# An FFT filter and an MLP on one core: where the forward second stage keeps its sums, and what its four filter products read

## The chip, the cores and the metric

The kernel runs on one core of a Trainium2 chip. The metric is the time of one execution in device microseconds (us), taken as the median of several runs. The time before is 2332.32 us, the median of 3 runs (2330.84 to 2332.87).

## The reference

Two things are computed one after the other. The first is a filter in the frequency domain along the sequence, for 8 batches of 3008 positions and 256 columns. The second is an MLP with 2048 hidden units on the resulting 24064 rows:

```python
def _attn_ref(x, filt_r, filt_i):
    X = np.fft.rfft(x, axis=1)
    F = (filt_r + 1j * filt_i)[None, :, :]
    y = np.fft.irfft(X * F, n=x.shape[1], axis=1)
    return y.astype(np.float32)

def _moe_ref(x, w_in, w_out):
    h = x @ w_in
    g = h * (1.0 / (1.0 + np.exp(-1.702 * h)))
    return (g @ w_out).astype(np.float32)
```

All arrays are float32. The weights of the MLP come as float64 and are converted on the chip.

## The kernel before

**Split numbers.** TensorE multiplies in float32r. To keep the precision, a value is split in a high half (ScalarE's copy rounded to float32r) and a low half (value less high half), and a product is made of the three products high x high, high x low, low x high.

**The transform.** 3008 = 64 x 47, so that the Fourier transform of one batch is done in two stages and the way back in two more. Stage 1 of batch b (`fft(b)`, lines 519 to 555) takes the input in 6 slices and writes `a_d` in DRAM. The second stage, `forward(i)` and `backward(i)` for i from 0 to 15 (lines 602 to 639), takes slice i of `a_d` (tile `zy`, high halves on 48 of 64 partitions in one half of the tile, low halves in the other), transforms it, multiplies it with the filter and transforms it back. The last stage belongs to the tiles of the MLP (below).

`forward(i)` works on two halves k = 0, 1 (real and imaginary part; `sides(k)` gives the 48 partitions h of the half, 0 to 47 or 64 to 111, and the 48 partitions o of the other half). `second(i, ..., k)` is one matmul that leaves two parts of the sum on the partitions h and o of one PSUM tile of 128x512. `merge` brings them together: ScalarE copies the part on o into the SBUF tile `c_buf` on h (L599), and VectorE adds the part on h, from PSUM, into `c_buf` (L600). Then four products with the filter `f_buf` are made: k = 0 times the imaginary part into `u_buf` (L608), k = 1 times the negative imaginary part into `u_buf` (L613), and both halves times the real part in one operation on 112 partitions (L614). GpSimd adds the two (L615), VectorE and GpSimd split the result in high and low half in `zy` (L619, L620). `backward(i)` does the same matmuls and merges with the inverse table, into the SBUF tile `b`, and every second one sends `b` to DRAM (`b_d`, L636) on ScalarE's queue.

**The MLP.** There are 48 tiles (b, t), six of each batch, of 512 columns (t = 5 of an even batch: 384), and each runs 16 chunks fc of 128 hidden units. A chunk has 6 matmuls into `h` (`first`, L844), two gelus of ScalarE, the first into `gh` in SBUF (L848), the second in place in PSUM (L849), VectorE's difference `gl` (L850), and 6 matmuls into `o` (`second` of `mlp`, L869). The 6 matmuls into `h` read the tile's `y` in high half (4 of them) and low half (2).

**Where a tile comes from.** `y` of tile (b, t) is made by `turned_signal`: load `br` from `b_d` (SyncE's queue), ScalarE's high halves `bh` and GpSimd's low halves `bl` (L785, L786), 6 matmuls, a transposition by VectorE, a trip through DRAM (`z_d`), and again high and low halves (L726, L727). That is so for t > 0 from batch 1 on and for t = 0 from batch 3 on; the other tiles go a shorter way (`signal`), and the tiles of batch 7 with t > 0 a packed one. Batch 0 has a transform of its own (`first_fft`), whose filter products (`product`, L457, L458) read a PSUM tile and the filter in SBUF. The load of `br` needs all 16 slices of the second stage of the batch, up to its last matmul, which the program names i2_b_15_1 (i2: way back, batch b, i = 15, k = 1). Names with s2 are the forward matmuls, s1 those of stage 1.

**PSUM.** Eight banks are shared by tags. `ring("f")` has three banks in turn for everything of the transforms, `ring("h")` two for `h`, `ps_o` has two for `o`, and `ps_x` is one that goes to "f" between chunks 32 and 95 of the whole program and to "h" after that.

**What sets the order.** The main loop runs over the chunks. Between chunks it advances the generators: `fft` of the next batch by a list of costs (`COSTS`, spread evenly over the chunks of one batch), and the generators of the next tiles by a table of due times. A scheduler that simulates a timeline then lays out each engine's instructions in one fixed order; matmuls given to `keep_in_program_order` (here those of the transforms) keep their order among themselves, others may move past them. On the chip each engine runs its list in that order and waits where an operand isn't there.

Of the kernel before, what the change touches and what calls it, by code (L numbers as in the profile page):

```python
# [14 lines left out]
ALU = mybir.AluOpType  # L15
# [6 lines left out]
Q = 112  # L22
# [147 lines left out]
def tile_kernel(  # L170
# [9 lines left out]
    nc = tc.nc  # L180
# [17 lines left out]
    def ring(kind, shape, name):  # L198

        own = {"f": (ps_f, 3), "h": (ps_h, 2)}[kind]  # L200
        turn_of[kind] += 1
        if shared[0] == kind and turn_of[kind] % (own[1] + 1) == 0:
            return ps_x.tile(shape, F32, tag="x", name=name)
        return own[0].tile(shape, F32, tag=kind, name=name)
# [99 lines left out]
    zy = []  # L304
# [157 lines left out]
    def fft(b):  # L462
# [111 lines left out]
        def load(i):  # L574
            for k in range(2):
                src = a_d[k, 4 * i : 4 * i + 4].rearrange("q n d -> n q d")
                nc.gpsimd.dma_start(zy[0][64 * k : 64 * k + 48, i % 2].rearrange("p k s d -> p (k s) d"), src)  # L577

        def load_f(i):
            for k in range(2):  # L580
                load_in(f_buf[64 * k : 64 * k + 48, 2 * (i % 2) : 2 * (i % 2) + 2], fs[i])

        def second(i, m, src, name, k):

            pin = tc.keep_in_program_order
            ps = ring("f", [P, 2, D], f"{name}_{b}_{i}_{k}")
            if i == 0:
                pin(nc.tensor.matmul(ps[:, 0], de_sb[:, k, m + 1], src[:, k, 0], start=True, stop=True))
                nc.tensor.matmul(ps[:, 1], de_sb[:, k, m], src[:, k, 1], start=True, stop=True)
            else:  # L590
                pin(nc.tensor.matmul(ps, de_sb[:, k, m], src[:, k], start=True, stop=True))  # L591
            return ps

        def sides(k):
            return slice(64 * k, 64 * k + 48), slice(64 - 64 * k, 112 - 64 * k)

        def merge(k, ps, dst):
            h, o = sides(k)
            nc.scalar.copy(dst[h], ps[o])  # L599
            nc.vector.tensor_tensor(dst[h], ps[h], dst[h], ALU.add)  # L600

        def forward(i):

            u1, u2 = c_buf[i % 3], u_buf[i % 2]
            fr = f_buf[:Q, 2 * (i % 2) : 2 * (i % 2) + 2]
            f_r, f_i = fr[:, :, 0, :], fr[:, :, 1, :]
            merge(0, second(i, 0, zy[0][:, i % 2], "s2", 0), u1)
            nc.vector.tensor_tensor(u2[64:Q], u1[0:48], f_i[0:48], ALU.mult)  # L608
            yield
            merge(1, second(i, 0, zy[0][:, i % 2], "s2", 1), u1)  # L610
            if i + 2 < 16:
                load(i + 2)
            nc.vector.scalar_tensor_tensor(u2[0:48], u1[64:Q], -1.0, f_i[64:Q], ALU.mult, ALU.mult)  # L613
            nc.vector.tensor_tensor(u1, u1[:Q], f_r, ALU.mult)  # L614
            nc.gpsimd.tensor_tensor(u1, u1, u2, ALU.add)  # L615
            y = zy[0][:, 2 + i % 2]
            for k in range(2):
                h, o = sides(k)
                nc.vector.tensor_copy(y[h, k], u1[h])  # L619
                nc.gpsimd.tensor_tensor(y[o, k], u1[h], y[h, k].bitcast(F32), ALU.subtract)  # L620
            if i + 2 < 16:
                load_f(i + 2)
            yield
# [24 lines left out]
        for i in range(17):  # L648
            if i < 16:
                yield from forward(i)  # L650
            if i:
                yield from backward(i - 1)
# [367 lines left out]
```

## Time and profile before

| | before |
|---|---|
| time, median of 3 runs | 2332.32 us (2330.84 to 2332.87) |
| the profiled execution | 2332.26 us, of which the span on the core 2330.2 us |
| granted clock of TensorE, mean | 1.00 |
| busy: TensorE | 2321.9 us, 100% |
| busy: VectorE | 1622.9 us, 70% |
| busy: ScalarE | 1458.4 us, 63% |
| busy: GpSimd | 1155.2 us, 50% |
| DMA | 293.44 MB, mean 126 GB/s |

PE is TensorE's matmuls, PEld its weight loads (which lie beside matmuls), DVE is VectorE, ACT ScalarE, POOL GpSimd, SP SyncE; ACTq and SPq are the queues on which these engines issue DMAs. A busy time is the sum of an engine's instructions over the span of 2330.2 us. L613 is line 613 of the kernel. "1155.2 x1019" is 1155.2 us in 1019 instructions. The profiled execution is one run of its own and stands 0.06 us from the median.

### The profile page before, as it was taken

What the parts mean: (1) busy time and instruction counts of PE and PEld (TensorE: products, weight loads), DVE (VectorE), ACT (ScalarE), POOL (GpSimd) and SP (SyncE); (2) the same over time, 40 slices, a digit from 0 to 9 for tenths busy, and PEclk for the clock granted to TensorE, in tenths of its full rate; (3) what the DMA queues carried; (4) which work ended last, traced back from release to release, by engine and by line L of the source; (5) the groups of instructions that cost most, each with busy time, mean ns of one, the idle gap of its engine ahead of it and who ended that gap; (6) DMA issues with size and microseconds to landing.
All of it is one profiled execution on the core that took longest, in us unless ns stands there. A gap on an engine that the chain in (4) does not pass through costs nothing.

```text
span 2330.2 us, 32285 instructions
## 1 busy us (share of the span) xinstructions
PE 2321.9 (100%) x10620; PEld 1942.6 (83%) x10620; DVE 1622.9 (70%) x2426; ACT 1458.4 (63%) x2686; POOL 1155.2 (50%) x1019
## 2 busy tenths in 40 slices
PE   9999999999999999999999999999999999999999
PEld 7888898888888889888888888988888888888887
DVE  7978876688666885678856887568876688633332
ACT  6666667666675666756676666766657566555553
POOL 3035546466564665556654555636647365422220
PEclk9999999999999999999999999999999999999999
DMA  9265545556455654555545554555655465421200
GB/s 340 82 193 110 111 107 143 133 136 134 108 148 128 144 136 131 152 121 138 133 133 141 130 128 121 148 136 128 138 133 143 115 141 121 111 62 55 82 28 19
DMA packets 191958, 293.44 MB, mean 126 GB/s; under 512 B 18736, under 2 KB 127920, under 8 KB 191792
## 3 DMA queue, kind: packets, MB, share of 16 engines
q1 hardware_dynamic: 115088, 180.89, 27.1%
q0 software_dynamic: 46592, 44.05, 11.6%
q10 hardware_dynamic: 30112, 66.44, 11.1%
q8 instruction: 85, 1.39, 0.3%
q14 instruction: 81, 0.66, 0.1%
HBM read 176.49 MB, written 114.82 MB: 125 GB/s over the span
## 4 chain that ended last, share of the span: by engine, by line
PE 95%; DVE 2%; DMA 2%; ACT 1%; issue 1%; ACTq 0%; POOL 0%; SPq 0%; DVEq 0%; POOLq 0%
PE h L844 43%; PE o L869 43%; PE i L591 2%; PE s L591 2%; PE s L540 1%; PE i L309 1%; PE i L307 1%; PE i L308 1%; PE i L709 1%; DMA x<-in_x_dram 0%; DVE gl L850 0%; PE s L388 0%; DVE w_tu L277 0%; DMA fs<-f_y 0%; DMA w<-in_w_out_dram 0%
## 5 line engine op out<-in xcount | busy, mean ns | idle before, releaser
L844 PE MATMUL h<-y,wi 128*128 128x512 f32 (+1 forms) x4608 | 1178.2, 385 | 0.6 <-DVE gl L850 0.5
L844 PEld LDWEIGHTS h<-y,wi 128*128 128x128 f32 x4608 | 858.9, 188 | 166.0 <-DVE gl L850 1.9
L850 DVE TENSOR_TENSOR gl<-h,gh 128x512 fp32r<-128x512 f32 (+1 forms) x768 | 521.3, 679 | 487.4 <-ACT h L849 452.9
L869 PE MATMUL o<-gh,wo 128*128 128x512 f32 (+1 forms) x3072 | 838.7, 385 | 0.8 <-ACT gh L848 0.8
L848 ACT ACTIVATE gh<-h 128x512 fp32r<-128x512 f32 (+1 forms) x768 | 452.7, 589 | 583.7 <-PE h L844 448.5
L869 PEld LDWEIGHTS o<-gh,wo 128*128 128x128 f32 x3072 | 573.4, 188 | 111.2 <-ACT gh L848 1.5
L869 PE MATMUL o<-gl,wo 128*128 128x512 f32 (+1 forms) x1536 | 481.7, 385 | 0.5 <-DVE gl L850 0.5
L849 ACT ACTIVATE h<-h 128x512 f32<-128x512 f32 (+1 forms) x768 | 448.4, 584 | 0.0
L620 POOL TENSOR_TENSOR zy<-c_buf,zy 48x512 fp32r<-48x512 f32 x224 | 316.3, 1412 | 75.0 <-DVE zy L619 62.7
L869 PEld LDWEIGHTS o<-gl,wo 128*128 128x128 f32 x1536 | 287.5, 188 | 56.4 <-DVE gl L850 1.2
L615 POOL TENSOR_TENSOR c_buf<-c_buf,u_buf 112x512 f32<-112x512 f32 x112 | 144.8, 1293 | 229.8 <-DVE c_buf L614 229.8
L577 POOL DMA_DIRECT2D zy<-a_d x224 | 130.7, 588 | 232.0 <-PE s L591 92.5
L786 POOL TENSOR_TENSOR bl<-br,bh 128x512 fp32r<-128x512 f32 x70 | 94.5, 1363 | 201.5 <-ACT bh L785 168.5
L600 DVE TENSOR_TENSOR c_buf<-s,c_buf 48x512 f32<-48x512 f32 x224 | 154.1, 688 | 34.0 <-ACT c_buf L599 29.4
L599 ACT COPY c_buf<-s 48x512 f32<-48x512 f32 x224 | 130.4, 582 | 70.8 <-PE s L591 57.6
L599 ACT COPY b<-i 48x512 f32<-48x512 f32 x224 | 130.4, 582 | 58.2 <-PE i L591 46.4
L600 DVE TENSOR_TENSOR b<-i,b 48x512 f32<-48x512 f32 x224 | 153.8, 687 | 15.1 <-ACT b L599 10.2
L543 DVE TENSOR_TENSOR a<-s,a 64x512 f32<-64x512 f32 x144 | 99.0, 688 | 61.9 <-ACT a L542 58.7
L619 DVE CAST zy<-c_buf 48x512 fp32r<-48x512 f32 x224 | 109.7, 490 | 39.1 <-POOL c_buf L615 34.1
L727 POOL TENSOR_TENSOR y<-y 128x512 fp32r<-128x512 f32 (+1 forms) x76 | 92.6, 1225 | 59.5 <-ACT y L726 48.1
L608 DVE TENSOR_TENSOR u_buf<-c_buf,f_buf 48x512 f32<-48x512 f32 x112 | 109.2, 975 | 3.8
L542 ACT CAST a<-s 64x512 fp32r<-64x512 f32 x144 | 83.8, 582 | 40.7 <-PE s L540 28.6
(138 smaller groups left out, 1867.4 us busy)
## 6 DMA issues: line engine op xcount, KB each, us to landing
f_buf<-fs SPq DMA_DIRECT2D x224, 192.0 KB, 3.5
zy<-a_d POOLq DMA_DIRECT2D x224, 192.0 KB, 3.7
a_d<-a ACTq DMA_DIRECT2D x144, 256.0 KB, 3.0
x<-in_x_dram SPq DMA_DIRECT2D x47, 512.0 KB, 5.5
br<-b_d SPq DMA_DIRECT2D x94, 256.0 KB, 4.5
out_dram<-out SPq DMA_DIRECT2D x43, 512.0 KB, 3.5
b_d<-b ACTq DMA_DIRECT2D x112, 192.0 KB, 2.8
z_d<-zt SPq DMA_DIRECT2D x40, 512.0 KB, 2.7
```

Of the source, the lines that this page charges most:

```text
L577: nc.gpsimd.dma_start(zy[0][64 * k : 64 * k + 48, i % 2].rearrange("p k s d -> p (k s) d"), src)
L599: nc.scalar.copy(dst[h], ps[o])
L600: nc.vector.tensor_tensor(dst[h], ps[h], dst[h], ALU.add)
L608: nc.vector.tensor_tensor(u2[64:Q], u1[0:48], f_i[0:48], ALU.mult)
L615: nc.gpsimd.tensor_tensor(u1, u1, u2, ALU.add)
L619: nc.vector.tensor_copy(y[h, k], u1[h])
L620: nc.gpsimd.tensor_tensor(y[o, k], u1[h], y[h, k].bitcast(F32), ALU.subtract)
L844: ins = nc.tensor.matmul(ps[:, :w], wi_sb[half][:, wk, kc, c], y[:, yk, kc, :w], start=n == 0, stop=n == 5)
L848: nc.scalar.activation(gh[:, :w], ps[:, :w], AF.Gelu_apprx_sigmoid)
L849: gelu.append(nc.scalar.activation(ps[:, :w], ps[:, :w], AF.Gelu_apprx_sigmoid).ins)
L850: nc.vector.tensor_tensor(gl[:, :w], ps[:, :w], gh[:, :w].bitcast(F32), ALU.subtract)
L869: ins = nc.tensor.matmul(pos[m][:, :w], wb[:, P * m : P * m + P], g[:, :w], start=first_one, stop=last_one)
```

## The change

`forward(i)` no longer calls `merge`. For each half, ScalarE copies the part on the other partitions into `c_buf` as before, but VectorE's sum now goes to the PSUM tile itself, over the part that it reads (L611 after). The four products are now four instructions of 48 partitions, two right behind each sum, and read the sum in PSUM and the filter in SBUF: times the imaginary part (L613 for k = 1, L615 for k = 0) and times the real part (L616), which replaces the one product on 112 partitions. The rest of the step (`load`, GpSimd's sum, the split, `backward`) is unchanged, though the load of the slice i + 2 is now asked for behind the products. Lines from 621 on of the kernel after are those of before plus 6.

```diff
--- before.py
+++ after.py
@@ -604,14 +604,20 @@
             u1, u2 = c_buf[i % 3], u_buf[i % 2]
             fr = f_buf[:Q, 2 * (i % 2) : 2 * (i % 2) + 2]
             f_r, f_i = fr[:, :, 0, :], fr[:, :, 1, :]
-            merge(0, second(i, 0, zy[0][:, i % 2], "s2", 0), u1)
-            nc.vector.tensor_tensor(u2[64:Q], u1[0:48], f_i[0:48], ALU.mult)
-            yield
-            merge(1, second(i, 0, zy[0][:, i % 2], "s2", 1), u1)
+            for k in range(2):
+                h, o = sides(k)
+                ps = second(i, 0, zy[0][:, i % 2], "s2", k)
+                nc.scalar.copy(u1[h], ps[o])
+                nc.vector.tensor_tensor(ps[h], ps[h], u1[h], ALU.add)
+                if k:
+                    nc.vector.scalar_tensor_tensor(u2[o], ps[h], -1.0, f_i[h], ALU.mult, ALU.mult)
+                else:
+                    nc.vector.tensor_tensor(u2[o], ps[h], f_i[h], ALU.mult)
+                nc.vector.tensor_tensor(u1[h], ps[h], f_r[h], ALU.mult)
+                if k == 0:
+                    yield
             if i + 2 < 16:
                 load(i + 2)
-            nc.vector.scalar_tensor_tensor(u2[0:48], u1[64:Q], -1.0, f_i[64:Q], ALU.mult, ALU.mult)
-            nc.vector.tensor_tensor(u1, u1[:Q], f_r, ALU.mult)
             nc.gpsimd.tensor_tensor(u1, u1, u2, ALU.add)
             y = zy[0][:, 2 + i % 2]
             for k in range(2):
```

In the lists of instructions, the rows below show operation, outputs <- inputs and shape. In them a name has the batch, the slice or chunk, and the half in it: s2_3_10_0 is the PSUM tile of batch 3, slice 10, half 0; h_2_5_7 is chunk 7 of tile (2, 5). The last number is a running one. "x4" is four alike in a row.

VectorE, forward step i = 10 of batch 3, before:

```order
L600 TENSOR_TENSOR c_buf1_83<-s2_3_10_0_7825,c_buf1_83 48x512
L608 TENSOR_TENSOR u_buf0_85<-c_buf1_83,f_buf_81 48x512
L850 TENSOR_TENSOR gl_2_3_12_7873<-h_2_3_12_7865,gh_2_3_12_7872 128x512
L600 TENSOR_TENSOR c_buf1_83<-s2_3_10_1_7848,c_buf1_83 48x512
L613 SCALAR_TENSOR_TENSOR u_buf0_85<-c_buf1_83,f_buf_81 48x512
L850 TENSOR_TENSOR gl_2_3_13_7901<-h_2_3_13_7893,gh_2_3_13_7900 128x512
L614 TENSOR_TENSOR c_buf1_83<-c_buf1_83,f_buf_81 112x512
```

The same step after:

```order
L611 TENSOR_TENSOR s2_3_10_0_7867<-s2_3_10_0_7867,c_buf1_83 48x512
L611 TENSOR_TENSOR s2_3_10_1_7891<-s2_3_10_1_7891,c_buf1_83 48x512
L615 TENSOR_TENSOR u_buf0_85<-s2_3_10_0_7867,f_buf_81 48x512
L616 TENSOR_TENSOR c_buf1_83<-s2_3_10_0_7867,f_buf_81 48x512
L613 SCALAR_TENSOR_TENSOR u_buf0_85<-s2_3_10_1_7891,f_buf_81 48x512
L616 TENSOR_TENSOR c_buf1_83<-s2_3_10_1_7891,f_buf_81 48x512
L856 TENSOR_TENSOR gl_2_3_15_8007<-h_2_3_15_7999,gh_2_3_15_8006 128x512
```

The products now hold the PSUM tile, here both sums stand ahead of them, and the step stands beside a later chunk of tile (2, 3).

TensorE, around the last matmul of the second stage of batch 3 (i2_3_15_1), before:

```order
L844 MATMUL h_2_5_1_8451<-y_2_5_7889,wi_0_583 128x384 x4
L869 MATMUL o_2_4_0_8069<-gl_2_4_14_8395,wo_1_984 128x512
L869 MATMUL o_2_4_0_8069<-gh_2_4_15_8422,wo_1_984 128x512
L591 MATMUL i2_3_15_1_8409<-zy_1451,de_sb_79 128x512
L869 MATMUL o_2_4_0_8069<-gh_2_4_15_8422,wo_1_984 128x512
```

The same matmul after:

```order
L875 MATMUL o_2_5_0_8543<-gh_2_5_4_8575,wo_0_584 128x384
L875 MATMUL o_2_5_1_8544<-gh_2_5_4_8575,wo_0_584 128x384
L850 MATMUL h_2_5_7_8644<-y_2_5_7932,wi_0_583 128x384 x4
L591 MATMUL i2_3_15_1_8457<-zy_1451,de_sb_79 128x512
L850 MATMUL h_2_5_7_8644<-y_2_5_7932,wi_0_583 128x384 x2
```

It stood among the matmuls of chunk 1 of tile (2, 5) and of the end of tile (2, 4); it stands within chunk 7 of tile (2, 5).

TensorE, where the first chunk of tile (3, 0) begins (h_3_0_0; its first 4 matmuls read the high half of y, the other 2 the low half), before:

```order
L540 MATMUL s1_4_2_1_8829<-e1_4_2_8752,t1_two_3258 128x512
L844 MATMUL h_3_0_0_8842<-y_3_0_8479,wi_0_583 128x512
L869 MATMUL o_2_5_0_8495<-gl_2_5_13_8769,wo_1_984 128x384
L869 MATMUL o_2_5_1_8496<-gl_2_5_13_8769,wo_1_984 128x384
L869 MATMUL o_2_5_0_8495<-gh_2_5_14_8788,wo_1_984 128x384
L869 MATMUL o_2_5_1_8496<-gh_2_5_14_8788,wo_1_984 128x384
L869 MATMUL o_2_5_0_8495<-gh_2_5_14_8788,wo_1_984 128x384
L869 MATMUL o_2_5_1_8496<-gh_2_5_14_8788,wo_1_984 128x384
L844 MATMUL h_3_0_0_8842<-y_3_0_8479,wi_0_583 128x512 x3
L844 MATMUL h_3_0_1_8868<-y_3_0_8479,wi_0_583 128x512 x4
```

After:

```order
L875 MATMUL o_2_5_0_8543<-gl_2_5_15_8867,wo_1_984 128x384
L875 MATMUL o_2_5_1_8544<-gl_2_5_15_8867,wo_1_984 128x384
L540 MATMUL s1_4_2_0_8848<-e0_4_2_8773,t1_two_3274 128x512
L540 MATMUL s1_4_2_1_8877<-e1_4_2_8800,t1_two_3274 128x512
L850 MATMUL h_3_0_0_8890<-y_3_0_8527,wi_0_583 128x512
L850 MATMUL h_3_0_1_8916<-y_3_0_8527,wi_0_583 128x512
L850 MATMUL h_3_0_2_8955<-y_3_0_8527,wi_0_583 128x512
L540 MATMUL s1_4_3_0_8940<-e0_4_3_8853,t1_two_3274 128x512
L850 MATMUL h_3_0_0_8890<-y_3_0_8527,wi_0_583 128x512 x3
L850 MATMUL h_3_0_1_8916<-y_3_0_8527,wi_0_583 128x512 x3
L850 MATMUL h_3_0_2_8955<-y_3_0_8527,wi_0_583 128x512 x3
L850 MATMUL h_3_0_0_8890<-y_3_0_8527,wi_0_583 128x512 x2
```

Before, the last two chunks of tile (2, 5) still stood around the first matmuls of tile (3, 0); after, tile (2, 5) is through, and three chunks of tile (3, 0) are begun with their high halves ahead of the first matmul on the low half. From i2_3_15_1 to that matmul there are, before, 20 matmuls of 512 columns and 172 of 384, and after, 17 and 118. On GpSimd, 16 operations stand before from the first bl of tile (3, 0) to its first L727 (L733 after), and 15 after; to the second one it is 17 in both.

The number of matmuls, of operations of ScalarE and GpSimd and of DMAs is unchanged; VectorE has 112 operations more.

## Rows read from the trace of the kernel before

**Rows 1.** Page, busy us (share of the span) and instructions, by engine.

```profile
PE 2321.9 (100%) x10620; PEld 1942.6 (83%) x10620; DVE 1622.9 (70%) x2426; ACT 1458.4 (63%) x2686; POOL 1155.2 (50%) x1019
```

**Rows 2.** TensorE's waits, first and last of 7: us, times, longest.

```profile
PE idle L328 <- DVE zero L375: 1.1, 1, 1.1
...
PE s L588 <- DMA zy<-a_d: 0.2, 1, 0.2
```

**Rows 3.** Window of the second stage: busy (instructions) by engine, PEclk, DMA share, GB/s.

```profile
1000.00:1145.00 145.00, 145.00 (x645) 120.16 (x644) 125.17 (x181) 91.99 (x166) 88.47 (x81) 1.00 0.59 133
```

**Rows 4.** VectorE by line and form: out<-in, count | busy us, mean ns | idle before.

```profile
L600 DVE TENSOR_TENSOR c_buf<-s,c_buf 48x512 f32<-48x512 f32 x224 | 154.1, 688 | 34.0 <-ACT c_buf L599 29.4
...
L608 DVE TENSOR_TENSOR u_buf<-c_buf,f_buf 48x512 f32<-48x512 f32 x112 | 109.2, 975 | 3.8
...
L613 DVE SCALAR_TENSOR_TENSOR u_buf<-c_buf,f_buf 48x512 f32<-48x512 f32 x112 | 88.8, 793 | 3.4
...
L614 DVE TENSOR_TENSOR c_buf<-c_buf,f_buf 112x512 f32<-112x512 f32 x112 | 85.2, 760 | 1.9
...
L457 DVE SCALAR_TENSOR_TENSOR u_buf<-s,f_y 48x512 f32<-48x512 f32 x8 | 5.5, 693 | 0.2
...
L458 DVE TENSOR_TENSOR u_buf<-s,f_y 48x512 f32<-48x512 f32 x8 | 5.5, 684 | 0.2
```

**Rows 5.** Page, costliest groups: ScalarE's gelu in place in PSUM.

```profile
L849 ACT ACTIVATE h<-h 128x512 f32<-128x512 f32 (+1 forms) x768 | 448.4, 584 | 0.0
```

**Rows 6.** TensorE's timeline at the start of batch 3: start, us, operation, count.

```profile
889.53 3.31 PE L844 MATMUL h<-y,wi 128*128 128x384 f32 x18
892.67 0.51 PE L869 MATMUL o<-gh,wo 128*128 128x384 f32 x2
...
922.49 1.78 PE L844 MATMUL h<-y,wi 128*128 128x512 f32 x7
924.10 0.51 PE L869 MATMUL o<-gl,wo 128*128 128x384 f32 x2
924.45 1.08 PE L844 MATMUL h<-y,wi 128*128 128x512 f32 x4
```

**Rows 7.** Timeline of all engines there; in brackets idle time before and its releaser.

```profile
887.91 0.40 PE L591 MATMUL i<-zy,de_sb 128*128 128x512 f32 x1
...
888.54 0.58 ACT L599 COPY b<-i 48x512 f32<-48x512 f32 x1
...
890.17 0.31 ACTq L636 DMA_DIRECT2D b_d<-b  x1
...
892.78 1.28 SPq L210 DMA_DIRECT2D br<-b_d  x2
...
897.38 1.14 ACT L785 CAST bh<-br 128x512 fp32r<-128x512 f32 x2 [1.40 <-DMA br<-b_d]
...
898.13 1.29 POOL L786 TENSOR_TENSOR bl<-br,bh 128x512 fp32r<-128x512 f32 x1 [13.64 <-ACT bh L785]
```

**Rows 8.** GpSimd's timeline at the starts of batches 3, 4, 5 and 6.

```profile
919.66 2.55 POOL L727 TENSOR_TENSOR y<-y 128x512 fp32r<-128x512 f32 x2
...
1180.12 2.55 POOL L786 TENSOR_TENSOR bl<-br,bh 128x512 fp32r<-128x512 f32 x2 [13.62 <-ACT bh L785]
...
1203.10 1.29 POOL L529 TENSOR_TENSOR e<-x,e 64x512 fp32r<-64x512 f32 x1 [0.62 <-ACT e L528]
...
1488.68 2.54 POOL L727 TENSOR_TENSOR y<-y 128x512 fp32r<-128x512 f32 x2
...
1747.66 2.55 POOL L786 TENSOR_TENSOR bl<-br,bh 128x512 fp32r<-128x512 f32 x2 [12.27 <-ACT bh L785]
```

**Rows 9.** TensorE's timeline: the last second-stage matmul of batches 4, 5 and 6.

```profile
1168.67 0.39 PE L591 MATMUL i<-zy,de_sb 128*128 128x512 f32 x1
...
1456.56 0.40 PE L591 MATMUL i<-zy,de_sb 128*128 128x512 f32 x1
...
1737.56 0.39 PE L591 MATMUL i<-zy,de_sb 128*128 128x512 f32 x1
```

## Prediction

> **What bounds the kernel now.** I read the busy table first, then who waited for whom, then the second stage's own windows, and last the timelines around the few places where a new batch of outputs begins. In the busy table TensorE is occupied for 2321.9 of 2330.2 us [rows 1]. "Busy" there is modelled, so I looked at its waits: the list of everything TensorE ever waited for has seven lines, from 1.1 down to 0.2 us, 3.7 us together [rows 2], and all are in the first 210 us or so. After that every matmul follows the one before it. So the time is the number of matmuls, which the change leaves alone, plus whatever waits on TensorE the change creates. There is next to nothing to win: at most those 3.7 us, and most of them lie ahead of the first instruction whose place changes. The question is only whether TensorE is made to wait.
>
> VectorE is the engine that the edit touches. In a stretch of the second stage it is busy 125.17 of 145 us, with TensorE busy for all 145 [rows 3]. It is loaded, not the bound.
>
> **The arithmetic of one iteration.** Before, one forward step costs VectorE two sums from PSUM (2 x 688 ns), L608 (975), L613 (793) and L614 over both halves at once (760): 3904 ns [rows 4]. After, the same two sums write to PSUM, and four products of 48x512 read PSUM and one SBUF tile. The first batch's product has just that form: L458 took 684 ns and L457 took 693 [rows 4]. No row has VectorE writing PSUM; the nearest is ScalarE's gelu in place, 584 ns to PSUM [rows 5], below VectorE's 688 to SBUF, and from above the slowest mean of the forward step, 975. I take 688, because this price was set by the 512 columns in every row without a second SBUF input. Sum: 2 x 688 + 684 + 693 + 2 x 684 = 4121 ns, 0.22 us more per iteration, 24 us over 112 iterations (with 975 for a sum: 0.79 us more). In the 145 us stretch, with 11 iterations, that is 2.4 us: VectorE goes from 86 to 88% (to 92% at the upper end). All of it lies beside TensorE's matmuls, so it counts zero; were VectorE full, it would be paid in waits. The copies, the add on GpSimd, the loads and the queues keep their number. The load of the next slice stands ahead of fewer products than before, and waits for none of them; zero.
>
> **The PSUM bank.** The tile of a half is now held through two products more. In the new order up to four other VectorE operations stand between a half's sum and its last reader: copy 0.58, then six operations of 0.69, 4.7 us after the matmul. The next matmul into the same bank (third in the ring) comes at least 25 matmuls later there, 5.7 us at 0.23 us each [rows 6], and 7 us or more in nine of ten cases. Covered, by 1 us at the tightest; no wait counted.
>
> **What the order does.** The scheduler lays the engines' orders out anew, and there lies the cost. TensorE's order is fixed when the program is built, and TensorE never idles, so a matmul that stands later in it runs later. Over a batch the second stage slides back in TensorE's order, most in the transform of batch 3. Its last matmul, i2_3_15_1, stood beside the gelu work of chunk 1 of tile (2,5), and now stands beside chunk 7, while the first chunk of tile (3,0), which is made from its result, has not moved away with it.
>
> What that chain takes is in the trace [rows 7, 8]: matmul at 887.91, copy, sum, store of b (890.17), load of br (892.78), bh at 897.38, GpSimd's bl at 898.13. GpSimd had stood idle 13.64 us for it; then it works through 16 operations in order, the next transform's butterflies among them, until the two L727 at 919.66 make the low half of y. They end at 920.95 and 922.21: 33.0 and 34.3 us behind the matmul. TensorE wanted them at 922.49 and 924.45 [rows 6], so the slack was 1.5 and 2.2 us.
>
> What the new order leaves: ahead of the first matmul on the low half there were 20 matmuls of 512 columns (the last one of the transform included) and 172 of 384; now 17 and 118. The price of one is 0.174 us at 384 columns (18 from 889.53 to 892.67) and 0.230 at 512 (7 from 922.49 to 924.10) [rows 6]. Check on the old order: 20 x 0.230 + 172 x 0.174 = 34.5, measured 34.6. New: 17 x 0.230 + 118 x 0.174 = 24.4 us. For the second low half: 26 and 118, 26.5 us. GpSimd has 15 operations instead of 16 ahead of the first L727, at 21.53 / 16 = 1.35 us, and 17 as before ahead of the second. So the chain needs 31.7 and 34.3 us and gets 24.4 and 26.5. TensorE waits 7.3 us at the first, and 7.8 in all after the second. A gelu now stands between the two bh, which adds 0.3 to the chain; behind the wait bh of tile (3,1) comes 0.2 late, since no work of tile (2,5) is left as cover. Together **8.3 us** at this place. The next transform's matmuls that also come too early here (s1_4_2, s1_4_3) wait within the same interval.
>
> Same sum at the other batch starts. Batch 4: the transform's last matmul at 1168.67, bl at 1180.12, and the 17th operation at 1203.10, so 1.436 us each with its waits [rows 8, 9]; 16 operations to the first L727 give 35.7 us, to the second (18th) 38.4; the order leaves 154 and 165 matmuls of 0.228, 35.1 and 37.6. Wait **0.8**. Batch 6 has the same order, but its bl came 10.1 us behind the matmul (1737.56 to 1747.66) instead of 11.45 [rows 8, 9]: 0. Batch 5: from 1456.56 to the end of the first L727, 1488.68 + 1.29, 33.4 us [rows 8, 9]; left are 15 x 0.230 + 169 x 0.174 = 32.9. Wait **0.5**. Batches 2 and 7 keep 1 to 2 us of slack by the same count: 0.
>
> Sum: 8.3 + 0.8 + 0.5 = 9.6 us. Nothing takes it back, since TensorE has no idle time behind it. The profiled execution took 2332.26 us, 0.06 under the median of the runs shown: 2332.26 + 9.6 = 2341.9 us, +0.41%.
>
> **The rivals.** *The slide costs nothing.* If the chain behind i2_3_15_1 is under 4.7 us late instead of 8, the result is 2332 to 2337 us, no difference that can be measured (0.2%, about what a measurement of this kernel can tell, is 4.7 us). For it: GpSimd's rows are rough, and its gaps of 0.07 us between operations could close, 1.2 us over 17. Against it: the DMA part alone (892.78 to 897.38) and 15 operations of 1.29 busy are no slack to take. 15%.
>
> *The banks come free late.* From the point where a half's copy, sum and products take over 5.7 us, TensorE waits in the second stage itself. At 975 ns for each write into PSUM the tightest hold of 4.7 us becomes 5.3, and 0.2 to 0.5 us at one place in ten of 224 would be 5 to 11 us on top: 2347 to 2353 us. Against it: every VectorE row with PSUM is 684 to 693 [rows 4]. 7%. The Trainium skill, PSUM — Partial Sum Buffer, summary of rules, says "Evacuate promptly — 2 MiB is tight", which is this rival's rule; the trace has no late bank to show for it.
>
> *The second stage gets faster and so does the kernel.* L608 took 975 ns on average from SBUF, where the same product from PSUM took 684 [rows 4]; if the calmer ports let GpSimd end its chain early too, TensorE still has only the 3.7 us of rows 2 to give back: 2329 to 2331 us. Its price is capped by TensorE's full row. 2%. The Trainium skill, SBUF — State Buffer, section "Who interferes with whom", has the rule: an operation of VectorE with two SBUF inputs contends with GpSimd's reads, one with a single SBUF input doesn't. The rows of L608 and L458 agree with it; but at the place that costs, VectorE runs no such pair, so GpSimd's 1.35 us there should stay.
>
> That the sums don't stay in PSUM is excluded by the order: the products name s2 as their input.
>
> **How the numbers follow.** 76% for the forecast, between 2337 and 2346 us (bounds: bl up to 2 us sooner or later, and the restart from 0 to 2), 15% for the slide at no cost, 7% for late banks, 2% for faster. The likeliest gives 2341.9. The range takes in the forecast, the upper part of the harmless slide and the lower part of the late banks: 2336 to 2349. Slower by over 0.2%: 76 + 7 = 83%; within: 15%; faster: 2%.
>
> **What would show it.** In the profile after, TensorE's list of waits gains lines at L850 (the old L844) on L733, and its timeline a gap of about 8 us near 925, where i2_3_15_1 runs at about 900; gaps under 1 us near 1220 and 1500. The products should read 684 to 693 ns, VectorE's stretch about 88%. If TensorE waits instead for VectorE at L591 throughout the stage, the bank was the cause. If it never waits, my reading of GpSimd's fixed order was wrong.

## The result

The changed kernel took 2351.73 us (median; 2349.53 to 2353.89) against 2332.6 us before: 1.0083 of it, with a 95% interval of 1.0066 to 1.0101. It is 19.1 us slower. The forecast was 2341.9 us, between 2336 and 2349: the sign was right, the forecast loss of 9.6 us was half of the measured one, and the time lies 2.7 us above the range. The profiled execution took 2351.61 us, 19.35 more than the one before, and is what the rows below are from. L727, L786, L844 and L869 of before are L733, L792, L850 and L875 here.

The page's first line of the kernel after, which answers [rows 1] (busy us, share, instructions):

```profile
PE 2331.7 (99%) x10620; PEld 1943.1 (83%) x10620; DVE 1658.3 (71%) x2538; ACT 1457.5 (62%) x2686; POOL 1140.8 (49%) x1019
```

The same matmuls, 10 us more of busy time for TensorE, and 99% instead of 100%: a part of the loss is idle time, another is matmuls that took longer. TensorE's waits in the kernel after, which answer [rows 2] (us in total, times, longest):

```profile
PE o L875 <- DVE out L883: 3.0, 2, 1.7
PE s L540 <- DVE a L544: 2.3, 3, 1.6
PE h L850 <- DVE gl L856: 2.3, 3, 1.4
PE h L850 <- POOL y L733: 1.5, 1, 1.5
PE o L875 <- ACT gh L854: 1.2, 4, 0.6
...
PE i L591 <- DVE c_buf L616: 0.8, 1, 0.8
```

Only one of these lines is the one that the prediction named (L733). To see where the 19 us lie, I added up for TensorE, matmul by matmul, by how much the step to the next start exceeds the pitch of its columns (0.227 us at 512, 0.173 at 384). That counts idle time and slow matmuls alike. Before, no step behind 210 us exceeds its pitch by more than 0.1 us, and the sum is below 1 us. After, the sum is 19.6 us larger. The table has it by place, with the value of before in the same stretch taken off; the columns e1 to e11 are the experiments below (e7 without the time of its added matmuls).

| stretch, us | what is there | after | e1 | e2 | e5 | e6 | e7 | e8 | e10 | e11 |
|---|---|---|---|---|---|---|---|---|---|---|
| 210 to 380 | second stage of batch 1 | 3.2 | 2.3 | 2.6 | 3.4 | 0.0 | 3.4 | 2.8 | 0.0 | 4.0 |
| 820 to 870 | second stage of batch 3 | 0.0 | 0.0 | 1.5 | 0.0 | 0.0 | 0.0 | 4.6 | 0.0 | 0.0 |
| 870 to 912 | its last matmuls | 1.8 | -0.1 | -0.2 | 0.0 | 2.4 | 1.6 | 2.3 | 0.0 | 1.9 |
| 912 to 955 | first chunks of tile (3,0) | 9.3 | 0.9 | 0.3 | 0.0 | 9.2 | 1.5 | 2.1 | 0.9 | 8.9 |
| 1160 to 1205, 1730 to 1785 | last matmuls of batches 4 and 6 | 0.0 | 2.4 | 0.0 | 0.0 | 0.0 | 0.0 | 0.0 | 2.7 | 0.0 |
| 1205 to 1245 | first chunks of tile (4,0) | 2.9 | 0.0 | 1.3 | 0.0 | 0.0 | 1.7 | 0.0 | 0.0 | 0.3 |
| 1480 to 1530 | first chunks of tile (5,0) | 0.6 | -0.1 | 0.4 | 0.0 | 0.1 | 0.6 | 0.2 | 0.0 | 0.4 |
| 1785 to 1825 | first chunks of tile (6,0) | 2.2 | 0.0 | 2.5 | 0.0 | 0.0 | 1.8 | 0.0 | 0.0 | 0.3 |
| all behind 210 us | | 19.6 | 5.7 | 8.6 | 3.3 | 11.5 | 10.3 | 11.9 | 3.4 | 15.4 |

The largest place, 9.3 us, is the one that was forecast at 8.3. Some 10 us more lie at five places, of which the prediction had two, at 0.8 and 0.5 us.

**The forecast place.** TensorE's timeline of the kernel after, from the last matmul of the second stage of batch 3 (start, us, operation, count, idle time before and its releaser), which answers [rows 6, 7]:

```profile
905.10 0.39 PE L591 MATMUL i<-zy,de_sb 128*128 128x512 f32 x1
...
930.48 0.47 PE L540 MATMUL s<-e,t_two 128*128 128x512 f32 x1 [1.65 <-DVE a L544]
931.20 0.76 PE L540 MATMUL s<-e,t_two 128*128 128x512 f32 x1 [0.25 <-DVE a L544]
...
936.24 6.07 PE L850 MATMUL h<-y,wi 128*128 128x512 f32 x15 [1.53 <-POOL y L733]
942.15 1.08 PE L875 MATMUL o<-gh,wo 128*128 128x512 f32 x4
```

and GpSimd's there, which answers [rows 8]:

```profile
914.75 2.54 POOL L792 TENSOR_TENSOR bl<-br,bh 128x512 fp32r<-128x512 f32 x2 [10.93 <-ACT bh L791]
...
934.92 1.26 POOL L733 TENSOR_TENSOR y<-y 128x512 fp32r<-128x512 f32 x1
...
937.38 1.27 POOL L733 TENSOR_TENSOR y<-y 128x512 fp32r<-128x512 f32 x1
```

The chain is as it was worked out: 15 operations from 914.75 to 934.92 are 1.345 us each (forecast 1.35), and the first low half is there 31.1 us behind the matmul at 905.10 (forecast 31.7), while the order leaves 24.4 us of matmuls. So it comes 6.7 us late. (The matmul that waits for it is the second of chunk 0. By the code the second and the fifth of a chunk's six read the low half, not the last two as the part on the change has it; the counts of matmuls are right.) The rows show what the sum had left out: once it had waited, TensorE ran slowly. The 15 matmuls that start at 936.24 need 5.91 us up to the next start at 942.15, where 15 x 0.227 = 3.4 us is the pitch: 2.5 us more. 6.7 + 2.5 is 9.2 of the 9.3 us lost. The windows of the kernel after (length; busy us and count of PE, PEld, DVE, ACT, POOL; granted clock; DMA share; GB/s):

```profile
920.00:930.00 10.00, 8.67 (x47) 7.77 (x45) 4.94 (x9) 7.88 (x15) 9.46 (x8) 1.00 0.62 200
930.00:936.00 6.00, 3.56 (x6) 1.59 (x6) 5.71 (x10) 3.90 (x8) 5.69 (x5) 0.59 1.02 310
936.00:941.00 5.00, 4.76 (x11) 3.80 (x12) 1.36 (x2) 0.00 (x0) 2.65 (x3) 0.50 0.74 203
941.00:950.00 9.00, 9.00 (x40) 7.19 (x40) 4.86 (x7) 8.51 (x16) 4.67 (x4) 0.98 0.13 28
```

The granted clock is 1.00 up to 930, then 0.59 and 0.50, and back at 0.98; 0.50 is the lower of the two levels (1.2 instead of 2.4 GHz). In the trace it fell at 931.1 us, after TensorE had stood still for 0.16 and 1.65 us and while it stood again for 0.25 us, and was back at 941.3 us, after TensorE had run without a wait from 936.24 on.

**The places that were not forecast.** First, ScalarE's timeline of the kernel after, before the wait of 0.77 us at 895 us, and from the timelines of VectorE and TensorE the end of that wait:

```profile
885.44 1.19 ACT L599 COPY b<-i 48x512 f32<-48x512 f32 x2
891.01 0.31 ACTq L642 DMA_DIRECT2D b_d<-b  x1
891.42 0.49 ACT L854 ACTIVATE gh<-h 128x384 fp32r<-128x384 f32 x1 [4.79 <-PE o L875]
891.74 0.31 ACTq L642 DMA_DIRECT2D b_d<-b  x1
891.81 0.49 ACT L855 ACTIVATE h<-h 128x384 f32<-128x384 f32 x1
892.32 0.58 ACT L610 COPY c_buf<-s 48x512 f32<-48x512 f32 x1
...
894.36 0.68 DVE L616 TENSOR_TENSOR c_buf<-s,f_buf 48x512 f32<-48x512 f32 x1
...
895.19 0.47 PE L591 MATMUL i<-zy,de_sb 128*128 128x512 f32 x1 [0.77 <-DVE c_buf L616]
```

The profile puts ScalarE's 4.79 us of idle time down to TensorE, which had long been done. ScalarE stood before the store L642, which waits until VectorE has ended the sum that it stores (L600, 890.31 to 891.71 for the two). Behind the store stand two gelus and the copy L610 of a half whose matmul had run at 887.47. So that half's bank was held until 895.04, 7.6 us instead of the 4.7 that I had counted from the matmul on. (e11 below shows that the store is not all of it.) Then ScalarE and VectorE before the wait at 1232 us (the rows of one engine, then the other, then TensorE):

```profile
1228.76 0.58 ACT L542 CAST a<-s 64x512 fp32r<-64x512 f32 x1 [0.54 <-ACT a L542]
1230.17 2.01 ACTq L470 DMA_DIRECT2D a_d<-a  x2
1232.28 0.58 ACT L542 CAST a<-s 64x512 fp32r<-64x512 f32 x1 [2.94 <-PE s L540]
...
1230.84 0.68 DVE L544 TENSOR_TENSOR a<-a,s 64x512 fp32r<-64x512 f32 x1
...
1233.50 0.67 DVE L883 COPY out<-o 128x512 f32<-128x512 f32 x1
...
1234.32 0.70 PE L875 MATMUL o<-gh,wo 128*128 128x512 f32 x2 [1.75 <-DVE out L883]
```

It is the same pattern: two stores of `a` stand in ScalarE's order, and wait for VectorE's L544. Behind them waits the copy L542 of a matmul that had run at 1229.23; behind that, on VectorE, L543 and then the copy L883 that empties a bank of `o`; and TensorE wants that bank. At 1805 us the rows repeat, 571.4 us later. Before, the matmuls of stage 1 ran 2.5 to 5.2 us apart here; after, there are pairs of them, 0.45 us apart at 1215 and 0.68 at 1222, and their copies, sums and stores come in bunches. Before, ScalarE's longest pause ahead of such a copy from 1205 to 1240 us is 1.09 us, and ends with the matmul, not with a store. The Trainium skill, DMA: Bandwidth & Descriptors, section "Anatomy of one DMA — SWDGE (gpsimd) path", says that a DMA's wait for a semaphore happens on the sequencer that issues it; the 4.79 us agree with it, here on ScalarE's queue.

Last, VectorE's timeline before the wait of 1.45 us at 219.08 us, in batch 1:

```profile
213.30 0.69 DVE L856 TENSOR_TENSOR gl<-h,gh 128x512 fp32r<-128x512 f32 x1
214.02 1.43 DVE L611 TENSOR_TENSOR s<-s,c_buf 48x512 f32<-48x512 f32 x2
...
217.60 0.69 DVE L616 TENSOR_TENSOR c_buf<-s,f_buf 48x512 f32<-48x512 f32 x1
218.33 0.69 DVE L856 TENSOR_TENSOR gl<-h,gh 128x512 fp32r<-128x512 f32 x1
```

Two sums and four products stand in a row, 214.02 to 218.29, and the gelu difference behind them could have begun at 214.96, when ScalarE's second gelu ended. It ends at 219.02, and TensorE's next chunk, which needs that bank of `h`, starts at 219.08. This is read from the rows; no run has VectorE in another order with the rest as it is.

### The profile page after: what moved, and what is told of

The parts are those of the page before. It is cut to its first block, busy times and chain, and to the rows that moved or that the text cites. A ratio compares the mean times of both kernels' runs of the same rounds, so it can differ in the third digit from the quotient of the medians.

```text
span 2349.8 us, 32568 instructions
## 1 busy us (share of the span) xinstructions
PE 2331.7 (99%) x10620; PEld 1943.1 (83%) x10620; DVE 1658.3 (71%) x2538; ACT 1457.5 (62%) x2686; POOL 1140.8 (49%) x1019
## 4 chain that ended last, share of the span: by engine, by line
PE 89%; DVE 4%; ACT 2%; POOL 2%; DMA 2%; issue 1%; ACTq 0%; SPq 0%; POOLq 0%; DVEq 0%
PE h L850 40%; PE o L875 40%; PE i L591 2%; PE s L591 2%; PE s L540 1%; DVE gl L856 1%; POOL e L529 1%; PE i L309 1%; PE i L308 1%; PE i L307 1%; DMA br<-b_d 1%; PE s L388 0%; PE i L715 0%; PE i L428 0%; POOL ev L522 0%
## 5 line engine op out<-in xcount | busy, mean ns | idle before, releaser
L850 PE MATMUL h<-y,wi 128*128 128x512 f32 (+1 forms) x4608 | 1182.1, 386 | 4.1 <-DVE gl L856 2.3
L850 PEld LDWEIGHTS h<-y,wi 128*128 128x128 f32 x4608 | 860.5, 188 | 174.1 <-DVE gl L856 6.5
L875 PE MATMUL o<-gh,wo 128*128 128x512 f32 (+1 forms) x3072 | 841.7, 385 | 4.2 <-DVE out L883 3.0
L875 PEld LDWEIGHTS o<-gh,wo 128*128 128x128 f32 x3072 | 572.8, 188 | 116.1 <-ACT h L855 3.7
L875 PE MATMUL o<-gl,wo 128*128 128x512 f32 (+1 forms) x1536 | 485.6, 385 | 0.6 <-DVE gl L856 0.5
L875 PEld LDWEIGHTS o<-gl,wo 128*128 128x128 f32 x1536 | 287.3, 188 | 56.9 <-DVE gl L856 1.9
L611 DVE TENSOR_TENSOR s<-s,c_buf 48x512 f32<-48x512 f32 x224 | 156.9, 700 | 34.5 <-ACT c_buf L610 28.7
L792 POOL TENSOR_TENSOR bl<-br,bh 128x512 fp32r<-128x512 f32 x70 | 89.3, 1293 | 187.4 <-ACT bh L791 166.8
L610 ACT COPY c_buf<-s 48x512 f32<-48x512 f32 x224 | 130.4, 582 | 67.1 <-PE s L591 53.6
L600 DVE TENSOR_TENSOR b<-i,b 48x512 f32<-48x512 f32 x224 | 153.6, 686 | 19.3 <-ACT b L599 14.1
L616 DVE TENSOR_TENSOR c_buf<-s,f_buf 48x512 f32<-48x512 f32 x224 | 154.2, 688 | 3.0
L543 DVE TENSOR_TENSOR a<-s,a 64x512 f32<-64x512 f32 x144 | 98.9, 687 | 54.6 <-ACT a L542 53.0
L625 DVE CAST zy<-c_buf 48x512 fp32r<-48x512 f32 x224 | 116.9, 522 | 21.1 <-POOL c_buf L621 16.1
L733 POOL TENSOR_TENSOR y<-y 128x512 fp32r<-128x512 f32 (+1 forms) x76 | 90.0, 1190 | 58.0 <-ACT y L732 40.1
L542 ACT CAST a<-s 64x512 fp32r<-64x512 f32 x144 | 83.8, 582 | 43.5 <-PE s L540 32.1
```

The lines of the kernel that those rows point to most:

```text
L610: nc.scalar.copy(u1[h], ps[o])
L611: nc.vector.tensor_tensor(ps[h], ps[h], u1[h], ALU.add)
L616: nc.vector.tensor_tensor(u1[h], ps[h], f_r[h], ALU.mult)
L850: ins = nc.tensor.matmul(ps[:, :w], wi_sb[half][:, wk, kc, c], y[:, yk, kc, :w], start=n == 0, stop=n == 5)
L875: ins = nc.tensor.matmul(pos[m][:, :w], wb[:, P * m : P * m + P], g[:, :w], start=first_one, stop=last_one)
```

## The experiments

Each run stands against the kernel before on the same chip; 2332 us is its median in all of them.

**e1: the order of before, with the PSUM operands.** A table has, for each chunk, how many second-stage matmuls stood ahead of it before, and the chunk's first matmul is put behind the last of them:

```diff
...
+                if n == 0:
+                    first_one = ins
+            c = NFC * tiles.index((b, t)) + fc
+            n = min(sum(map(int, AHEAD[: c + 1])), len(passed_by))
+            if n and True:
+                order = mybir.DependencyInfo(mybir.DependencyClass.NoSync, mybir.DependencyReason.DATA)
+                tc.add_manual_dep(first_one.ins, passed_by[n - 1].ins.name, order, reason="behind the second stage")
...
```

> The changed kernel, with TensorE's order around the second stage held to that of the kernel before: the first matmul of each chunk is put behind as many second-stage matmuls as stood ahead of it before (where they are emitted by then). The sums stay in PSUM and the four products read them there. Theory 1 (the fixed order costs, not the PSUM operands): the waits at 895, 920 to 945, 1232 and 1805 us go; what is left is the order of VectorE near 217 and 320 us (up to 3 us): 2333 to 2337 us. Theory 2 (the PSUM operands cost, by VectorE's 112 more operations or by banks that come free late): TensorE waits for VectorE at the second stage's matmuls and at the gelu differences instead, all through the stage: 2345 us or more.

Measured: 2337.76 us, ratio 1.0025 (1.0016 to 1.0035). 14 of the 19 us go, with every sum and product still in PSUM. The waits in its profile that TensorE doesn't have before:

```profile
PE h L862 <- DVE gl L875: 1.7, 2, 1.4
PE i L602 <- POOL zy L638: 1.6, 2, 0.8
...
PE h L862 <- POOL y L745: 0.7, 1, 0.7
```

So the order of TensorE is what costs most, and the scheduler put the second stage's matmuls later than their operands needed. Not all of it, though: 1.6 us are second-stage matmuls that now stand as early as before and find their operand late, at the ends of batches 4 and 6 (2.4 us lost). I read that as a price of the longer step itself; VectorE's order was not held, so it isn't shown. And batch 1 still loses 2.3 of its 3.2 us. The time is 0.8 us over the range that was expected.

**e2: the same, only in the tiles (2,4) and (2,5).** The condition above is `if n and b == 2 and t >= 4`.

> The changed kernel, with TensorE's order held to that of before only in the tiles (2,4) and (2,5), where the second stage of batch 3 ends. Theory 1: only the losses from 890 to 945 us go (1.9 and 9.3 us of 19.4), those near 217, 320, 1232, 1509 and 1805 us stay: 2339 to 2343 us. Theory 2, or one in which a wait taken away here comes back later: 2347 us or more. If the other places were consequences of this one (later work thrown out of step), they would go too: 2333 to 2336 us.

Measured: 2340.57 us, ratio 1.0038 (1.0025 to 1.0051), as the first theory has it. The losses from 870 to 955 us go, and nearly all of those of the other batches stay (the table's column): the one near 1232 us falls from 2.9 to 1.3 us, and 1.5 us come anew before 870 us. So the others are not consequences of this one.

**e5 and e6: the change in one batch alone.** `forward` has the new lines `if b == 1` (e5) or `if b == 3` (e6), and the old ones otherwise.

> The change in batch 1 alone; the batches 2 to 7 are as before, and TensorE's order at their ends too. In the changed kernel TensorE lost 3.0 us from 210 to 340 us (1.7 near 217, 1.3 from 310 to 340). If places lose on their own: about 3 us, 2334 to 2337 us, and nothing lost behind 350 us. If the whole comes from the second stage of every batch in like shares: also about 3 us, but then a batch without a batch start that runs late (the next run) must cost no more.

> The change in batch 3 alone. The order at the end of its second stage is that of the changed kernel (24.3 us of matmuls from i2_3_15_1 to the first low half of tile (3,0)), the other batches are as before. If places lose on their own: 1.9 us near 895 and 9.3 us from 920 to 945 us, 11.2 in all: 2341 to 2345 us. If the cost were spread over the iterations: about 3 us, 2335 us.

Measured: e5 2334.97 us, ratio 1.0011 (1.0002 to 1.002), e6 2342.93 us, 1.0045 (1.003 to 1.0061). 2.9 and 10.9 us; by the table 3.3 and 11.5, at the places of the changed kernel and nowhere else. With the 5.7 us at the starts of batches 4, 5 and 6 that makes 20.5 of 19.6 us: the places add up. An iteration itself costs nothing that can be seen: batch 3 alone costs over three times what batch 1 does.

**e7: the wait filled with matmuls.**

```diff
...
+                for _ in range(36 if n == 0 and (b, t, fc) == (2, 5, 15) else 0):
+                    nc.tensor.matmul(ps[:, :w], wi_sb[half][:, wk, kc, c], y[:, yk, kc, :w], start=True, stop=True)
                 ins = nc.tensor.matmul(ps[:, :w], wi_sb[half][:, wk, kc, c], y[:, yk, kc, :w], start=n == 0, stop=n == 5)
```

> The changed kernel with 36 more matmuls of 384 columns (6.2 us at 0.173), repeats of the first matmul of chunk 15 of tile (2,5), which the real ones then overwrite. They stand ahead of the wait at the start of batch 3. There the chain comes 31.1 us behind i2_3_15_1 and the order leaves 24.4 us of matmuls: 6.7 us late; measured were 9.3 us lost, with a granted clock of 0.56 from 930 to 940 us. If the other 2.6 us are matmuls at the lower clock behind the wait: with the wait filled the granted clock stays at 1.00, and this place costs 6.2 to 7 us in all, 2 to 3 less than in the changed kernel: 2348 to 2350 us. If the chain itself was 9.3 us late, or the clock has nothing to do with it, the fill is only a part of the wait: 2351 to 2352 us. If TensorE wasn't waiting there at all: 2358 us.

Measured: 2348.03 us, ratio 1.0067 (1.0054 to 1.0079): 36 matmuls more, and 3.7 us faster than the changed kernel. The windows of this run:

```profile
920.00:930.00 10.00, 10.00 (x58) 9.83 (x57) 5.24 (x8) 6.90 (x13) 9.46 (x8) 1.00 0.64 196
930.00:940.00 10.00, 9.33 (x47) 7.91 (x46) 5.83 (x9) 5.33 (x11) 8.28 (x7) 1.00 0.82 221
940.00:950.00 10.00, 10.00 (x43) 7.84 (x44) 6.17 (x10) 9.20 (x18) 6.00 (x5) 1.00 0.37 98
```

The granted clock stays at 1.00. The place costs 6.2 us of fill and 1.5 of waits, 7.7 instead of 9.3. So the lower clock cost 1.6 us by this run, 2.5 by the matmuls' steps; the fill was 0.5 us short of the lateness, and a wait of 0.67 us for a gelu difference was still there. Another 1.6 us of the gain are the waits at 1232 and 1805 us, which came out shorter in this run, for no reason that the run shows.

**e8: the second stage asked for earlier.** In the line that sets the end of a batch's share, `18 if b > 1` is `18 + 8 if b > 1`.

> The changed kernel, with the second stage of batches 2 on asked for earlier (it is to end 26 instead of 18 quarter-tile widths ahead of the batch's first tile), so that i2_3_15_1 stands 34.2 us of matmuls ahead of the first low half of tile (3,0), as it did before (34.3). Theory 1: the 9.3 us from 920 to 945 us go, and the waits at 1232, 1509 and 1805 us too; but the second stage's last matmuls now come ahead of their operands and wait 2 to 4 us in the batches: 2338 to 2347 us. If not the place of i2_3_15_1 but the PSUM operands cost: 2350 us or more.

Measured: 2345.34 us, ratio 1.0054 (1.0041 to 1.0068). Within what the first theory has, and no cure: the starts of the batches lose 2.3 us instead of 15, but the second stage now runs ahead of its operands and loses 4.6 us from 820 to 870.

**e4: the same arithmetic, emitted where before has it.** The next load stands ahead of the second half's products, and both real products come last:

```diff
...
             if i + 2 < 16:
                 load(i + 2)
+            nc.vector.scalar_tensor_tensor(u2[0:48], s[1][64:Q], -1.0, f_i[64:Q], ALU.mult, ALU.mult)
+            for k in range(2):
+                h = sides(k)[0]
+                nc.vector.tensor_tensor(u1[h], s[k][h], f_r[h], ALU.mult)
...
```

> The changed kernel's arithmetic (sums in PSUM, four products reading them), but emitted where the kernel before emits them: the next load ahead of the products of the second half, both real products last. TensorE's order at the batch starts is that of the changed kernel (24.3 us of matmuls from i2_3_15_1 to the first low half of tile (3,0)). Theory 1: 2350 to 2353 us, the same waits from 920 to 945 us. If the place of the products or of the load is the cause: below 2345 us.

Measured: 2351.83 us, ratio 1.0084 (1.0069 to 1.0099), with 8.6 us lost from 912 to 955. The place of the products in the program is not the cause.

**e3 and e9: four products from SBUF.** `merge` is back, the products are the four of the change but read `c_buf`; e9 also has the order of before, as e1.

```diff
...
-                ps = second(i, 0, zy[0][:, i % 2], "s2", k)
-                nc.scalar.copy(u1[h], ps[o])
-                nc.vector.tensor_tensor(ps[h], ps[h], u1[h], ALU.add)
+                merge(k, second(i, 0, zy[0][:, i % 2], "s2", k), u1)
...
```

> The changed kernel's four products of 48 partitions, in its places in the program, but the sums go to SBUF as before and the products read them there. If the split in four and the new places of the products make the order slide: about 2350 us, like the changed kernel. If the PSUM operands make the scheduler slide the second stage: i2_3_15_1 stays 33.2 us of matmuls ahead of the first low half of tile (3,0) (34.3 before, 24.3 after), the chain of 31 to 33 us fits or is 1 us late there, and what it costs are VectorE's products with two SBUF operands (0.79 to 0.98 us each instead of 0.69) where it stands close in the stage of batch 1: 2335 to 2342 us.

> The four products from SBUF (sums in SBUF), with TensorE's order held to that of before in the same way as in the first run of this study. Without that hold it took 2352.4 us, and TensorE lost 17.9 us behind 210 us, most of it inside the second stages (3.7 us near 1080, 2.3 near 840, 2.1 near 1650, 2.5 near 1700). If the new layout of the order is what costs there too: 2336 to 2341 us, like the same hold with the sums in PSUM (2337.8). If VectorE's dearer products cost (two operands in SBUF: 1052, 764 and 785 ns instead of 684, 693 and 688, 0.6 us more in a step): 2346 us or more, with TensorE waiting for VectorE and GpSimd inside the second stages.

Measured: e3 2352.42 us, ratio 1.0086 (1.0071 to 1.0101), e9 2362.68 us, 1.013 (1.0115 to 1.0145). e3 has the time of its first case, but not for that reason: TensorE's order at the start of batch 3 stays near that of before (0.9 us lost there), and some 15 us go inside the second stages of batches 3, 4 and 6. In e9 the second case is true: with the order of before it gets worse by 10 us, where the PSUM form got better by 14. VectorE's groups in e3 (count, busy us, mean ns, idle before):

```profile
L614 DVE TENSOR_TENSOR c_buf<-c_buf,f_buf 48x512 f32<-48x512 f32 x224 | 175.9, 785 | 5.8
...
L613 DVE TENSOR_TENSOR u_buf<-c_buf,f_buf 48x512 f32<-48x512 f32 x112 | 117.9, 1052 | 3.8
L611 DVE SCALAR_TENSOR_TENSOR u_buf<-c_buf,f_buf 48x512 f32<-48x512 f32 x112 | 85.6, 764 | 3.5
```

A step costs VectorE 2 x 687 + 2 x 785 + 1052 + 764 = 4760 ns here, against 4153 in the changed kernel and 3904 before. There it is the second stage's own chain that TensorE waits for, which one sees in the waits of e9:

```profile
PE i L602 <- POOL zy L636: 8.9, 7, 2.0
PE h L860 <- DVE gl L873: 6.9, 8, 1.8
```

TensorE waits for `zy`, whose chain goes through VectorE and GpSimd, and for gelu differences. With 0.6 us less in a step, in PSUM, the same order costs some 6 us (e1).

**e10: batches 2 to 7 with the order of before, batch 1 as before.** e1 with the new lines `if b > 1`.

> The change in the batches 2 to 7 alone, with TensorE's order held to that of before. The same with the change in all batches took 2337.8 us, of which 2.6 us were lost from 210 to 340 us, in the stage of batch 1, 1.1 us near 925 and 2.4 us near 1170 and 1740 us. If these places are independent: 2.6 us less, 2334 to 2336 us, with the losses near 925, 1170 and 1740 us as they were. If the time of batch 1 was only handed on: 2337 to 2339 us.

Measured: 2336.12 us, ratio 1.0017 (1.0008 to 1.0027), 0.1 us over the first range that was expected. By the table batch 1's loss is gone and the 3.4 us of the rest stand as they were. This is the best of the forms that change more than one batch, and it doesn't reach the kernel before.

**e11: the stores off ScalarE's queue.**

```diff
-                nc.scalar.dma_start(*pair)
+                (nc.sync if b in (5, 7) else nc.scalar).dma_start(*pair)
...
-                        nc.scalar.dma_start(b_d[:, 32 * n + 4 * g : 32 * n + 4 * g + 4, :], be[64 * n : 64 * n + 48])
+                        (nc.sync if b == 3 and i == 13 else nc.scalar).dma_start(b_d[:, 32 * n + 4 * g : 32 * n + 4 * g + 4, :], be[64 * n : 64 * n + 48])
```

> The changed kernel with two kinds of stores put on SyncE's queue instead of ScalarE's: the store of b after i = 13 of batch 3 (L642), and the stores of the first stage of batches 5 and 7 (L470). VectorE's order is the same, TensorE's differs in some 20 rows near 1225 and 1797 us. In the changed kernel ScalarE stood before these stores until VectorE had ended what they carry (4.8 us up to 891.4, and from 1229.3 to 1232.3 and 1800.8 to 1803.7), and the copy out of the PSUM bank and the gelu stood behind them. If that is what costs 1.9 us near 895 and 2.7 and 2.2 us near 1232 and 1805: most of these 6.8 us go, 2345 to 2347 us, with the 9.3 us from 920 to 945 us and the 3.0 of batch 1 as they were. If VectorE itself is late there, the same time is lost at the same places: 2350 to 2352 us.

Measured: 2346.5 us, ratio 1.0058 (1.0041 to 1.0075), 5.2 us under the changed kernel. At the starts of batches 4 and 6, 4.5 of 5.1 us go. ScalarE there:

```profile
1229.65 0.58 ACT L542 CAST a<-s 64x512 fp32r<-64x512 f32 x1 [2.21 <-PE s L540]
1230.14 0.59 ACT L854 ACTIVATE gh<-h 128x512 fp32r<-128x512 f32 x1
```

The copy starts at 1229.65, right behind its matmul, instead of 1232.28. At 895 us the 1.9 us stay. VectorE and TensorE there, in e11:

```profile
893.55 0.69 DVE L611 TENSOR_TENSOR s<-s,c_buf 48x512 f32<-48x512 f32 x1
...
894.98 0.68 DVE L616 TENSOR_TENSOR c_buf<-s,f_buf 48x512 f32<-48x512 f32 x1
...
895.80 0.47 PE L591 MATMUL i<-zy,de_sb 128*128 128x512 f32 x1
```

The copy of the half came at 889.21 instead of 892.32, but VectorE's sum on it only at 893.55, since in VectorE's order two gelu differences, a split and two sums of `b` stand ahead of it. The bank, written at 888.65, was free at 895.66, and TensorE's matmul follows 0.14 us later. Another bank is late in this run: its last product ends at 888.54, and the matmul at 888.65 comes 0.45 us late. So the store is not what this place hangs on alone: VectorE's own row holds the banks too, and with the order of before (e1, e2) TensorE doesn't come for them too early. The 0.9 us for GpSimd's `zy` in this run's list of waits lie in batch 1, at 335 us, and belong to its 4.0 us. Some twenty rows of TensorE's order near 1225 and 1797 us differ in this run, so it isn't proved that the 4.5 us are the stores' wait alone.

## Why the prediction was wrong in size, and what of it was right

The sum had 9.6 us, at three places; 19.6 were lost. The rest is what it put at nothing or too low: VectorE's row in batch 1 (3.2 us instead of 0), the stores on ScalarE's queue at the starts of batches 4 and 6 (5.1 instead of 0.8), the bank at 895 us (1.8 instead of 0), and the start of batch 3 (9.3 instead of 8.3).

- **TensorE is the bound, and what matters is whether it waits**: right. Held to the order of before, the new arithmetic costs 5.7 of the 19.6 us.
- **The products' prices**: right. VectorE's groups of the kernel after, for [rows 4]:

```profile
L611 DVE TENSOR_TENSOR s<-s,c_buf 48x512 f32<-48x512 f32 x224 | 156.9, 700 | 34.5 <-ACT c_buf L610 28.7
L616 DVE TENSOR_TENSOR c_buf<-s,f_buf 48x512 f32<-48x512 f32 x224 | 154.2, 688 | 3.0
...
L613 DVE SCALAR_TENSOR_TENSOR u_buf<-s,f_buf 48x512 f32<-48x512 f32 x112 | 77.6, 693 | 3.6
L615 DVE TENSOR_TENSOR u_buf<-s,f_buf 48x512 f32<-48x512 f32 x112 | 76.6, 684 | 3.7
```

  A sum into PSUM takes 700 ns (taken: 688), the products 684, 693 and 688. A step is 4153 ns against 4121 forecast. VectorE's share in the stretch from 1000 to 1145 us was forecast at 88% and is 119.09 of 145 us, 82%: not that it is faster, but the stage had slid, and less of it lies in that stretch (25 of its sums instead of 29).
- **The slide at the start of batch 3**: right in mechanism and place, short in size. 8.3 us were forecast and 9.3 measured. The term that is missing is the clock: the sum priced each matmul behind the wait as if it had not waited. The lateness itself was 6.7 us, less than the 7.3 that the sum had at the first low half. The 1.0 us that it added for the second one, the gelu between and the late (3,1) didn't come: the second low half was there at 938.65, and at the lower clock TensorE came to it at 940.25.
- **"All of it lies beside TensorE's matmuls, so it counts zero"**: the step that failed first. In batch 1 it counts 3.3 us (e5), of which TensorE's order of before gives back little (e1: 2.3 left). The average load said nothing on the row of six operations that now stands ahead of a gelu difference. The order fence of VectorE in the part on the change shows the pattern, with gl between the products before and behind them after; I read it as a matter of VectorE's load, and didn't ask for when that gl was due.
- **"The queues keep their number"**: failed, and the costliest. Stores on ScalarE's queue wait for VectorE, and the gelu and the copies out of PSUM stand behind them. In the old order the sums were through when their stores came; when matmuls of the transforms drew together, they were not. This is how batches 4 and 6 lost 2.9 and 2.2 us instead of 0.8 and 0, as far as e11 shows it (4.5 of the 5.1 us go): there I followed only the chain of y, which has no wait at either.
- **"Covered, by 1 us at the tightest"** (the bank): failed at one place of 224, at 895 us, since the hold was counted with a ScalarE that copies at once and a VectorE that comes to the sum at once. Neither did: 7.6 us, and still 7.0 in e11, where the copy was on time. That rival had a price of 5 to 11 us on top, and late banks all over the stage; there are none.
- **Batch 5**: 0.5 forecast, 0.6 measured, and the wait is for the low half, as worked out: its first operation on GpSimd starts at 1507.90 and takes 1.3 us, and TensorE's matmul starts at 1509.26.
- **The range**: its upper end was set by bounds on the terms that I had, and left no room for terms that I had not. That the order had moved on every engine was a reason to leave some.

What stays open: how much of the loss at 895 us is the store and how much VectorE's own row, what in VectorE's order would cure batch 1, and why the waits at 1232 and 1805 us and those in batch 1 differ by up to 1 us between kernels whose order there is the same (e4, e7, e11).

## What to carry to other kernels

Where one engine is full and the orders are fixed when the program is built, an edit on another engine is priced by what it does to the order: first hold the old order (e1) and see what is left, then look at each place that moved. At each such place follow every engine's queue back, the stores that an engine issues for another one's data included, and not only the chain that seems the longest. And price a wait of TensorE with what follows it: here 6.7 us of lateness cost 9.3.

## What was not expected of the hardware

- A product of 48x512 with one operand in PSUM took 684 to 693 ns, with both in SBUF 764 to 1052 ns (e3), as means of each line. The fastest one from SBUF took 671 ns, so it is not the floor that is higher. In e3 two casts from SBUF to SBUF, which take 0.88 us for a pair elsewhere, took 3.20 us beside two operations of GpSimd:

```profile
1079.59 2.53 POOL L790 TENSOR_TENSOR bl<-br,bh 128x512 fp32r<-128x512 f32 x2
1079.66 3.20 DVE L623 CAST zy<-c_buf 48x512 fp32r<-48x512 f32 x2 [0.16 <-POOL c_buf L619]
```

  The Trainium skill, SBUF — State Buffer, section "Who interferes with whom", says that a cast may take the pair of ports that VectorE shares with GpSimd, and that whoever is later then stands still; 3.20 us beside 2.53 agree with it.
- Writing a sum into the PSUM tile that is read costs VectorE hardly more than writing it to SBUF: 700 ns against 688.
- The granted clock fell to 0.50 at the waits from 928 to 936 us, the longest of them 1.65 us, and cost 1.6 to 2.5 us there; at the waits of 1.45 us (219) and 1.75 us (1234) it stayed at 1.00.
